# Loading a chunk's inputs with one DMA per tensor into padded rows, in a gated linear attention with a maxout layer

## The chip, the cores and the metric

The kernel runs on one core of a Trainium2 chip. The metric is the time of one execution on the device in microseconds (us). Engines are named as in the profile: PE is TensorE (PEld its weight loads), DVE is VectorE, ACT is ScalarE, POOL is GpSimd, and SP is the queue from which all DMAs here are issued.

## The reference

The inputs are q, k, v and f_logit of shape (4, 8, 768, 48): batch, heads, time, head size. All are float32. The output is 3072 x 384.

```
f = sigmoid(f_logit)
for t in range(768):
    state = f[t][:, None] * state + outer(k[t], v[t])     # 48 x 48 per batch and head
    y[t]  = q[t] @ state
x   = y with the heads side by side                        # 3072 x 384
out = maximum(x @ w1, x @ w2) @ w_out                      # d_ff = 1024
```

## The kernel before, in words

Time is cut into 6 chunks of 128 steps. One chunk of one batch is a unit. Units are numbered i = 4 * chunk + batch, so there are 24, and the four batches of a chunk follow each other. All eight heads of a unit are worked on together, with time on the 128 partitions and 8 x 48 = 384 values in a row.

The stages of a unit are functions. `s_ell` takes the logarithm of the gate (two activations on ACT, tile `e` from `ft`, then `ell`) and casts v to bf16 (tile `vb` from `vt`, on DVE). `s_cum` sums the logarithms along time with a matmul (`cum`), takes exponentials (`ei`, `ed`, `fl` on ACT), and scales k and q with them on POOL (`kp`, `qp`). `s_tr` transposes kp and qp on PE and copies them out of PSUM on DVE (`trs`). `s_a` multiplies k with q per head on PE and masks the product on DVE (`am`). `s_y` updates the state (`sa` on PE, `tmp` on DVE, `st` on POOL) and computes y on PE, which ACT copies (`x`). `s_xT` transposes x for the dense layers (`xT`, copied on DVE).

The dense layers are written as max(a, b) = b + relu(a - b). So `d` is x times (w1 - w2), `gT` its relu on ACT, and `o` sums x times (w2 w_out) and gT times w_out. DVE copies o to `ob`, which has three buffers, and SP writes it out (line 178). This work is a list of small pieces that the unit loop takes from between its stages, four per iteration and two more in the early ones. The pieces of a chunk are put on the list when the chunk's last xT is done. The preparation of the weights (`w_h`, `wo`, `w2T`, `w2o`, `wd`) stands first on the same list.

The unit loop runs over i from -4 to 23. In iteration i it does `s_y(i)`, `s_tr(i + 2)`, `s_a(i + 1)`, `s_cum(i + 3)`, `s_xT(i)` and `s_ell(i + 4)`. The order of instructions on each engine is the order in which the program writes them. A manual schedule is set, so no planner moves them. An engine that waits holds up everything behind it.

The loads of a unit are four DMAs on SP, for f, k, q and v, of 192 KB each. The pool `loads` has five buffers for each tensor, so it holds five units. Before the loop the program issues units 0 to 2, the weights w2 and w_out, unit 3, w1, and unit 4. In the loop, `load(i + 8)` stands at the end of iteration i and reuses the buffers of unit i + 3. Each load first waits until the last reader of its buffer is done: e for f, kp for k, qp for q, vb for v. The output DMAs are in the same queue, in program order.

Of the kernel before, what the change touches and what calls it, by code (L numbers as in the profile page):

```python
# [11 lines left out]
F32 = mybir.dt.float32  # L12
BF16 = mybir.dt.bfloat16
AF = mybir.ActivationFunctionType
# [3 lines left out]
def kernel(  # L18
# [14 lines left out]
    nc = tc.nc  # L33
    B, H, S, D = q.shape
    C = 128
    nch = S // C
# [4 lines left out]
    DP = 64  # L41
    NP = H // 2
    T = nch * B
# [1 line left out]

    ctx.enter_context(tc.manual_schedule())
    consts = ctx.enter_context(tc.tile_pool(name="consts", bufs=1))
    loads = ctx.enter_context(tc.tile_pool(name="loads", bufs=5))
    work = ctx.enter_context(tc.tile_pool(name="work", bufs=2))
    ps_s = ctx.enter_context(tc.tile_pool(name="ps_s", bufs=3, space=bass.MemoryType.PSUM))  # L50
    ps_a = ctx.enter_context(tc.tile_pool(name="ps_a", bufs=1, space=bass.MemoryType.PSUM))
# [2 lines left out]
    nc.scalar.preload_act_table_set("natural_log_exp_and_others")  # L54


    ld = {}

    def load(i):
        c, b = divmod(i, B)  # L60
        sl = slice(c * C, (c + 1) * C)
        t = {}
        for name, src in (("f", f_logit), ("k", k), ("q", q), ("v", v)):
            t[name] = loads.tile([C, H, D], F32, name=f"{name}t", tag=f"{name}t")
            nc.sync.dma_start(out=t[name], in_=src[b, :, sl, :].rearrange("h p d -> p h d"))
        ld[i] = t

    w1_f = consts.tile([C, JG, d_ff], F32, name="w1_f")
    w2_f = consts.tile([C, JG, d_ff], F32, name="w2_f")
# [2 lines left out]
    for i in range(3):  # L72
        load(i)
    nc.sync.dma_start(out=w2_f, in_=moe_w2.rearrange("(j p) ff -> p j ff", p=C))
    nc.sync.dma_start(out=wo_f, in_=moe_w_out.rearrange("(j p) dm -> p j dm", p=C))
    load(3)
    nc.sync.dma_start(out=w1_f, in_=moe_w1.rearrange("(j p) ff -> p j ff", p=C))
    load(4)


    ut = consts.tile([C, C], BF16)
# [104 lines left out]
    def unit(n=1):  # L186
        for _ in range(n):
            if units:
                units.popleft()()


    st = {}

    def s_ell(i):
        t = ld[i]
        e = work.tile([C, dm], F32, name="e", tag="e")
        ell = ell_b[i % 2]
        nc.scalar.activation(e, t["f"].rearrange("p h d -> p (h d)"), AF.Exp, scale=-1.0)
        nc.scalar.activation(ell[:, :, 0:D], e.rearrange("p (h d) -> p h d", h=H), AF.Ln, bias=1.0)  # L199
        vb = work.tile([C, dm], BF16, name="vb", tag="vb", bufs=6)  # L200
        nc.vector.tensor_copy(vb, t["v"].rearrange("p h d -> p (h d)"))  # L201
        st[i] = {"ell": ell, "v": vb}

    def s_cum(i):
        s, t = st[i], ld[i]
        ell = s["ell"]
        ps = ps_s.tile([C, 512], F32, name="cum", tag="s")
        nc.tensor.matmul(out=ps[:, 0:dm], lhsT=ut, rhs=ell[:, :, 0:D], start=True, stop=True)  # L208
        for p in range(NP):
            nc.tensor.matmul(out=ps[:, dm + p:dm + p + 1],  # L210
                             lhsT=ell[:, 2 * p:2 * p + 2, :].rearrange("p h d -> p (h d)"),
                             rhs=ones_col, start=True, stop=True)
        ed = work.tile([C, dm], F32, name="ed", tag="ed")
        ei = work.tile([C, dm], F32, name="ei", tag="ei")
        fl = work.tile([C, NP], F32, name="fl", tag="fl", bufs=5)
        nc.scalar.activation(ei, ps[:, 0:dm], AF.Exp)  # L216
        nc.scalar.activation(ed, ps[:, 0:dm], AF.Exp, scale=-1.0)  # L217
        nc.scalar.activation(fl, ps[:, dm:dm + NP], AF.Exp, scale=-1.0)
        qp, kp = qp_b[i % NQ], kp_b[i % NQ]
        nc.gpsimd.tensor_mul(kp[:, :, 0:D], t["k"], ei.rearrange("p (h d) -> p h d", h=H))  # L220
        nc.gpsimd.tensor_mul(qp[:, :, 0:D], t["q"], ed.rearrange("p (h d) -> p h d", h=H))  # L221
        s.update(fl=fl, qp=qp, kp=kp)
        del ld[i]

    def s_tr(i):
        s = st[i]
        ps = ps_s.tile([C, 2, NP, C], BF16, name="tr", tag="s")
        for n, src in enumerate((s["kp"], s["qp"])):
            for p in range(NP):
                nc.tensor.transpose(out=ps[:, n, p, :],  # L230
                                    in_=src[:, 2 * p:2 * p + 2, :].rearrange("p h d -> p (h d)"),
                                    identity=ident)
        tr = work.tile([C, 2, NP, C], BF16, name="trs", tag="trs", bufs=3)
        nc.vector.tensor_copy(tr, ps)  # L234
        s["tr"] = tr

    def s_a(i):
        s = st[i]
        tr = s["tr"]

        ps = ps_a.tile([C, 2, NP, C], F32, name="a", tag="a")
        for p in range(NP):
            for o in range(2):
                r = slice(o * DP, o * DP + D)
                nc.tensor.matmul(out=ps[:, o, p, :], lhsT=tr[r, 0, p, :], rhs=tr[r, 1, p, :],  # L245
                                 start=True, stop=True)
        am = work.tile([C, 2, NP, C], BF16, name="am", tag="am")
        nc.vector.tensor_mul(am.rearrange("p o n c -> p (o n) c"),  # L248
                             ps.rearrange("p o n c -> p (o n) c"), mask)
        s["am"] = am  # L250

    def s_y(i):
        c, b = divmod(i, B)
        s = st[i]
        am, vb, tr = s["am"], s["v"], s["tr"]
        old, new = st_b[b][c % 2], st_b[b][(c + 1) % 2]
        if c < nch - 1:
            sa = ps_s.tile([C, NP, 2 * D], F32, name="sa", tag="s")
            for p in range(NP):
                nc.tensor.matmul(out=sa[:, p, :],  # L260
                                 lhsT=s["kp"][:, 2 * p:2 * p + 2, :].rearrange("p h d -> p (h d)"),
                                 rhs=vb[:, 2 * p * D:(2 * p + 2) * D], start=True, stop=True)
            tmp = work.tile([C, NP, 2 * D], F32, name="tmp", tag="tmp")
            nc.vector.tensor_add(tmp, sa, old)  # L264
            for o in range(2):
                r, e = slice(o * DP, (o + 1) * DP), slice(o * D, (o + 1) * D)
                nc.gpsimd.tensor_mul(new[r, :, e], tmp[r, :, e],  # L267
                                     s["fl"][r, :].unsqueeze(2).to_broadcast([DP, NP, D]))
        y = ps_s.tile([C, dm], F32, name="y", tag="s")
        for p in range(NP):  # L270
            if c > 0:
                nc.tensor.matmul(out=y[:, 2 * p * D:(2 * p + 2) * D], lhsT=tr[:, 1, p, :],  # L272
                                 rhs=old[:, p, :], start=True, stop=False)
            for o in range(2):
                h = 2 * p + o
                ds = slice(h * D, (h + 1) * D)
                nc.tensor.matmul(out=y[:, ds], lhsT=am[:, o, p, :], rhs=vb[:, ds],  # L277
                                 start=(c == 0), stop=(c == 0 or o == 1))
        x = work.tile([C, dm], BF16, name="x", tag="x")
        nc.scalar.copy(x, y)  # L280
        s["x"] = x

    def s_xT(i):
        c, b = divmod(i, B)
        s = st.pop(i)
        if b == 0:
            xT_g[c] = work.tile([C, JG, GT], BF16, name="xT", tag="xT", bufs=3)
        ps = ps_s.tile([C, JG, C], BF16, name="xtp", tag="s")
        for j in range(JG):
            nc.tensor.transpose(out=ps[:, j, :], in_=s["x"][:, j * C:(j + 1) * C], identity=ident)  # L290
        nc.vector.tensor_copy(xT_g[c][:, :, b * C:(b + 1) * C], ps)  # L291


    for i in range(-4, T):
        if i >= 0:
            s_y(i)
        unit()
        if 0 <= i + 2 < T:
            s_tr(i + 2)
        unit()  # L300
        if 0 <= i + 1 < T:
            s_a(i + 1)
        unit()
        if 0 <= i + 3 < T:
            s_cum(i + 3)
        unit()
        if i >= 0:
            s_xT(i)
        if i < B:
            unit()  # L310
            unit()
        if i >= 0 and i % B == B - 1:
            push_group(i // B)
        if 0 <= i + 4 < T:
            s_ell(i + 4)
        if 5 <= i + 8 < T:
            load(i + 8)
    while units:
        unit()

# [29 lines left out]
```

## Time and profile before

| what | value |
|---|---|
| median of 2 timed runs | 186.99 us (186.93 to 187.04) |
| profiled execution | 185.38 us |
| its span, first to last instruction | 183.6 us |
| mean granted TensorE clock | 0.944 |
| busy: PE, DVE, ACT, POOL | 138.6, 102.5, 86.1, 75.7 us |
| DMA: packets, bytes | 105154 packets, 28.56 MB, of which 100272 under 512 B |

All times in the lines of the profile count from the start of the span. The timed runs give the whole execution. The profiled execution has 1.8 us around its span. A line number such as L201 is that of the kernel before.

The lines of the changed kernel are shifted by 11 to 13. For example, the cast of v stands in line 201 before and in line 213 after.

### The profile page before, as it was taken

What the parts mean: (1) busy time and instruction counts of PE and PEld (TensorE: products, weight loads), DVE (VectorE), ACT (ScalarE), POOL (GpSimd) and SP (SyncE); (2) the same over time, 40 slices, a digit from 0 to 9 for tenths busy, and PEclk for the clock granted to TensorE, in tenths of its full rate; (3) what the DMA queues carried; (4) which work ended last, traced back from release to release, by engine and by line L of the source; (5) the groups of instructions that cost most, each with busy time, mean ns of one, the idle gap of its engine ahead of it and who ended that gap; (6) DMA issues with size and microseconds to landing.
All of it is one profiled execution on the core that took longest, in us unless ns stands there. A gap on an engine that the chain in (4) does not pass through costs nothing.

```text
span 183.6 us, 3633 instructions
## 1 busy us (share of the span) xinstructions
PE 138.6 (75%) x1373; PEld 85.4 (46%) x1384; DVE 102.5 (56%) x161; ACT 86.1 (47%) x200; POOL 75.7 (41%) x107
## 2 busy tenths in 40 slices
PE   0000208946778989999999998999899988998992
PEld 0000106534555545655456654665556654564560
DVE  8200605389777576686676676766776744452031
ACT  2000074483555675446744577346873376412700
POOL 8200004646666366544466544566544644000000
PEclk9999999985555999999999999999999999999999
DMA  6999999999999997698996999969801120022022
GB/s 114 194 185 347 373 199 362 186 187 171 194 189 190 164 191 131 165 209 174 195 151 164 215 172 186 172 142 216 152 0 43 50 86 0 4 87 86 0 89 86
DMA packets 105154, 28.56 MB, mean 156 GB/s; under 512 B 100272, under 2 KB 104368, under 8 KB 105136
## 3 DMA queue, kind: packets, MB, share of 16 engines
q1 hardware_dynamic: 105136, 28.32, 77.1%
q8 instruction: 11, 0.18, 0.5%
q14 instruction: 7, 0.06, 0.1%
HBM read 23.59 MB, written 4.72 MB: 154 GB/s over the span
## 4 chain that ended last, share of the span: by engine, by line
issue 39%; PE 32%; POOL 23%; ACT 3%; POOLq 1%; DVE 1%; ACTq 0%
PE o L172 13%; POOL qp L221 11%; POOL kp L220 9%; PE d L156 9%; PE tr L230 6%; PE a L245 2%; POOL st L98 1%; ACT ei L216 1%; PE y L272 1%; ACT ed L217 1%; PE y L277 1%; ACT gT L158 1%; POOLq L345 1%; POOL ell L94 0%; PE cum L208 0%
## 5 line engine op out<-in xcount | busy, mean ns | idle before, releaser
L220 POOL TENSOR_TENSOR kp<-kt,ei 128x384 bf16<-128x384 f32 x24 | 24.9, 1036 | 76.4 <-issue 38.9
L156 PE MATMUL d<-xT,wd 128*128 128x512 bf16 x133 | 36.7, 383 | 2.3 <-DVE xT L291 1.1
L158 ACT ACTIVATE gT<-d 128x512 bf16<-128x512 f32 x48 | 29.0, 605 | 19.0 <-PE d L156 18.5
L172 PE MATMUL o<-wo,gT 128*128 128x384 bf16 x192 | 37.7, 326 | 0.0
L234 DVE COPY trs<-tr 128x1024 bf16<-128x1024 bf16 x24 | 16.6, 692 | 25.8 <-PE tr L230 25.7
L248 DVE TENSOR_TENSOR am<-a,mask 128x1024 bf16<-128x1024 f32 x24 | 29.3, 1219 | 2.9 <-PE a L245 2.9
L216 ACT ACTIVATE ei<-cum 128x384 f32<-128x384 f32 x24 | 11.7, 489 | 38.2 <-PE cum L210 38.2
L221 POOL TENSOR_TENSOR qp<-qt,ed 128x384 bf16<-128x384 f32 x24 | 27.6, 1148 | 0.0
L176 DVE COPY ob<-o 128x384 f32<-128x384 f32 x24 | 13.4, 558 | 23.3 <-PE o L172 22.4
L172 PEld LDWEIGHTS <-gT 128*128 128x128 bf16 x192 | 17.8, 98 | 10.4
L267 POOL TENSOR_TENSOR st<-tmp,fl 64x192 bf16<-64x192 f32 x40 | 20.0, 501 | 2.3 <-DVE tmp L264 0.8
L124 PE MATMUL w2tp<-ident,w_h 128*128 128x128 bf16 x24 | 3.5, 308 | 21.0 <-DVE w_h L112 21.0
L201 DVE CAST vb<-vt 128x384 bf16<-128x384 f32 x24 | 16.9, 703 | 0.0
L156 PEld LDWEIGHTS <-wd 128*128 128x128 bf16 x144 | 11.8, 98 | 10.8 <-issue 2.3
L172 PE MATMUL o<-w2o,xT 128*128 128x384 bf16 x72 | 15.7, 327 | 0.0
L230 PE MATMUL tr<-ident,qp 128*128 128x128 bf16 x96 | 10.6, 239 | 5.8 <-POOL qp L221 5.0
L277 PE MATMUL y<-vb,am 128*128 128x48 bf16 x192 | 12.0, 190 | 2.2 <-DVE am L248 1.4
L116 ACT CAST wo<-wo_f 128x768 bf16<-128x768 f32 x4 | 3.1, 824 | 21.9 <-DMA wo_f<-in_moe_w_out_dram 21.9
L208 PE MATMUL cum<-ell,ut 128*128 128x384 bf16 x24 | 8.9, 369 | 6.0 <-ACT ell L199 6.0
L277 PEld LDWEIGHTS <-am 128*128 128x128 bf16 x192 | 10.3, 101 | 6.4 <-DVE xT L291 3.7
L280 ACT CAST x<-y 128x384 bf16<-128x384 f32 x24 | 11.2, 467 | 4.2 <-PE y L277 4.1
L199 ACT ACTIVATE ell<-e 128x384 bf16<-128x384 f32 x24 | 12.5, 523 | 0.9
(42 smaller groups left out, 185.1 us busy)
## 6 DMA issues: line engine op xcount, KB each, us to landing
ft<-in_f_logit_dram SPq DMA_DIRECT2D x24, 192.0 KB, 4.3
kt<-in_k_dram SPq DMA_DIRECT2D x24, 192.0 KB, 4.2
qt<-in_q_dram SPq DMA_DIRECT2D x24, 192.0 KB, 4.2
vt<-in_v_dram SPq DMA_DIRECT2D x24, 192.0 KB, 4.3
out_dram<-ob SPq DMA_DIRECT2D x24, 192.0 KB, 2.0
w_f<-in_moe_w_dram SPq DMA_DIRECT2D x2, 1536.0 KB, 7.7
wo_f<-in_moe_w_out_dram SPq DMA_DIRECT2D x1, 1536.0 KB, 11.0
```

The source lines that it names most:

```text
L156: nc.tensor.matmul(out=ps, lhsT=wd[:, j, f * C:(f + 1) * C], rhs=xT[:, j, :], start=(j == 0), stop=(j == JG - 1))
L158: nc.scalar.activation(gT[:, f, :], ps, AF.Relu)
L172: nc.tensor.matmul(out=ps, lhsT=mms[n][0], rhs=mms[n][1], start=(n == 0), stop=(n == len(mms) - 1))
L201: nc.vector.tensor_copy(vb, t["v"].rearrange("p h d -> p (h d)"))
L216: nc.scalar.activation(ei, ps[:, 0:dm], AF.Exp)
L220: nc.gpsimd.tensor_mul(kp[:, :, 0:D], t["k"], ei.rearrange("p (h d) -> p h d", h=H))
L221: nc.gpsimd.tensor_mul(qp[:, :, 0:D], t["q"], ed.rearrange("p (h d) -> p h d", h=H))
L230: nc.tensor.transpose(out=ps[:, n, p, :], in_=src[:, 2 * p:2 * p + 2, :].rearrange("p h d -> p (h d)"), identity=ident)
L234: nc.vector.tensor_copy(tr, ps)
L248: nc.vector.tensor_mul(am.rearrange("p o n c -> p (o n) c"), ps.rearrange("p o n c -> p (o n) c"), mask)
L267: nc.gpsimd.tensor_mul(new[r, :, e], tmp[r, :, e], s["fl"][r, :].unsqueeze(2).to_broadcast([DP, NP, D]))
L277: nc.tensor.matmul(out=y[:, ds], lhsT=am[:, o, p, :], rhs=vb[:, ds], start=(c == 0), stop=(c == 0 or o == 1))
```

## The change

The tiles of f, k, q and v now hold a whole chunk of all four batches, `[C, B, H, DP]`. DP is 64, so each row of 48 float32 values (192 bytes) lies in a slot of 256 bytes. The pool has two buffers for each tensor, two chunks in place of five units.

Chunk 0 is still loaded in four parts, unit by unit, in the old places among the weights. Every later chunk is loaded by `load_chunk` with one DMA for each tensor, in the order f, k, q, v. Each has 128 partitions x 32 rows x 48 values, 768 KB. Chunk 1 is issued after w1, where the load of unit 4 was. Chunk c + 2 is issued at the end of iteration 4c, the first of chunk c, and uses the buffers of chunk c. The compute instructions are the same in number and order on every engine. They read the tiles through views with a gap after each row of 48.

On SP the DMAs now stand in this order: chunk 0 and the weights, chunks 1, 2 and 3, four outputs, chunk 4, four outputs, chunk 5, and sixteen outputs.

```diff
-    loads = ctx.enter_context(tc.tile_pool(name="loads", bufs=5))
+    loads = ctx.enter_context(tc.tile_pool(name="loads", bufs=2))
...
-    ld = {}
+    SRC = (("f", f_logit), ("k", k), ("q", q), ("v", v))
+    ld_c = {n: {} for n, _ in SRC}
+
+    def load_one(name, src, c):
+        if c not in ld_c[name]:
+            ld_c[name][c] = loads.tile([C, B, H, DP], F32, name=f"{name}t", tag=f"{name}t")
+        return ld_c[name][c]
 
     def load(i):
         c, b = divmod(i, B)
         sl = slice(c * C, (c + 1) * C)
-        t = {}
-        for name, src in (("f", f_logit), ("k", k), ("q", q), ("v", v)):
-            t[name] = loads.tile([C, H, D], F32, name=f"{name}t", tag=f"{name}t")
-            nc.sync.dma_start(out=t[name], in_=src[b, :, sl, :].rearrange("h p d -> p h d"))
-        ld[i] = t
+        for name, src in SRC:
+            t = load_one(name, src, c)
+            nc.sync.dma_start(out=t[:, b, :, 0:D], in_=src[b, :, sl, :].rearrange("h p d -> p h d"))
+
+    def load_chunk(c):
+        sl = slice(c * C, (c + 1) * C)
+        for name, src in SRC:
+            t = load_one(name, src, c)
+            nc.sync.dma_start(out=t[:, :, :, 0:D].rearrange("p b h d -> p (b h) d"),
+                              in_=src[:, :, sl, :].rearrange("b h p d -> p (b h) d"))
...
-    load(4)
+    load_chunk(1)
...
     def s_ell(i):
-        t = ld[i]
+        c, b = divmod(i, B)
+        t = {n: ld_c[n][c][:, b, :, 0:D] for n in ld_c}
...
-        nc.scalar.activation(e, t["f"].rearrange("p h d -> p (h d)"), AF.Exp, scale=-1.0)
+        nc.scalar.activation(e.rearrange("p (h d) -> p h d", h=H), t["f"], AF.Exp, scale=-1.0)
...
-        nc.vector.tensor_copy(vb, t["v"].rearrange("p h d -> p (h d)"))
+        nc.vector.tensor_copy(vb.rearrange("p (h d) -> p h d", h=H), t["v"])
...
-        if 5 <= i + 8 < T:
-            load(i + 8)
+        if i >= 0 and i % B == 0 and i // B + 2 < nch:
+            load_chunk(i // B + 2)
```

More of the change, by code (lines that the diff above doesn't have):

```diff
@@ L194, in s_ell @@
     def s_ell(i):
-        t = ld[i]
+        c, b = divmod(i, B)
+        t = {n: ld_c[n][c][:, b, :, 0:D] for n in ld_c}
         e = work.tile([C, dm], F32, name="e", tag="e")
         ell = ell_b[i % 2]
-        nc.scalar.activation(e, t["f"].rearrange("p h d -> p (h d)"), AF.Exp, scale=-1.0)
+        nc.scalar.activation(e.rearrange("p (h d) -> p h d", h=H), t["f"], AF.Exp, scale=-1.0)
         nc.scalar.activation(ell[:, :, 0:D], e.rearrange("p (h d) -> p h d", h=H), AF.Ln, bias=1.0)
         vb = work.tile([C, dm], BF16, name="vb", tag="vb", bufs=6)
-        nc.vector.tensor_copy(vb, t["v"].rearrange("p h d -> p (h d)"))
+        nc.vector.tensor_copy(vb.rearrange("p (h d) -> p h d", h=H), t["v"])
         st[i] = {"ell": ell, "v": vb}
     def s_cum(i):
-        s, t = st[i], ld[i]
+        c, b = divmod(i, B)
+        s = st[i]
+        t = {n: ld_c[n][c][:, b, :, 0:D] for n in ld_c}
         ell = s["ell"]
@@ L222, in s_cum @@
         s.update(fl=fl, qp=qp, kp=kp)
-        del ld[i]
     def s_tr(i):
```

## The prediction

> **What bounds the kernel now.** I read the views in this order: the slices and the table of DMA issues on the page, to see whether the loads are the limit; the busy times by stretch, to see which engine limits each stage; the timelines of the queue that issues DMAs, of VectorE, GpSimd and ScalarE between 43 and 53 us, because that is where a load of a whole chunk would first be late; last the landing times of single loads.
>
> ```profile
> PEclk9999999985555999999999999999999999999999
> DMA  6999999999999997698996999969801120022022
> GB/s 114 194 185 347 373 199 362 186 187 171 194 189 190 164 191 131 165 209 174 195 151 164 215 172 186 172 142 216 152 0 43 50 86 0 4 87 86 0 89 86
> ...
> vt<-in_v_dram SPq DMA_DIRECT2D x24, 192.0 KB, 4.3
> out_dram<-ob SPq DMA_DIRECT2D x24, 192.0 KB, 2.0
> ```
>
> One slice is 183.6/40 = 4.59 us. The DMA engines are full for the first 15 slices (to 69 us) and fairly busy up to slice 28. PEclk is at half in slices 9 to 12 (41 to 60 us). So the loads could be the limit early, but busy is not the same as late. The stretches tell which stage is held by what (columns: length, busy time and instructions of PE, PEld, DVE, ACT, POOL, then clock, DMA share, GB/s):
>
> ```profile
> 32.00:36.50 4.50, 4.50 (x29) 2.65 (x28) 1.89 (x4) 1.90 (x5) 2.82 (x2) 1.00 1.25 186
> 50.00:54.50 4.50, 3.40 (x37) 2.34 (x36) 3.41 (x6) 2.23 (x7) 3.02 (x5) 0.50 1.39 193
> 75.00:97.50 22.50, 21.20 (x230) 13.05 (x230) 15.13 (x24) 13.40 (x34) 12.20 (x16) 1.00 0.94 175
> ```
>
> From 75 us on TensorE is busy for 21.20 of 22.50 us: this stage, four units (one chunk) long, is TensorE's, and loads only have to keep up. Between 41 and 59 us no engine is full. There the unit loop has a period of 4.51 us (kp starts at 44.69, 49.19 and, one period on, 53.70) and is a ring: kp and qp on GpSimd, their transposes on TensorE, cum behind them in TensorE's order, ei on ScalarE, and the next kp. These lines (start, length, and in brackets the idle time before and its releaser) are the end of unit iteration 0 and the beginning of iteration 1:
>
> ```profile
> 44.69 0.35 DVE L291 COPY xT<-xtp 128x384 bf16<-128x384 bf16 x1
> 44.95 0.95 DVE L201 CAST vb<-vt 128x384 bf16<-128x384 f32 x1
> 45.82 0.55 DVE L264 TENSOR_TENSOR tmp<-sa,st 128x384 f32<-128x384 f32 x1
> 47.45 0.69 DVE L234 COPY trs<-tr 128x1024 bf16<-128x1024 bf16 x1 [1.08 <-PE tr L230]
> ...
> 46.72 1.07 POOL L267 TENSOR_TENSOR st<-tmp,fl 64x192 bf16<-64x192 f32 x2
> 49.19 1.00 POOL L220 TENSOR_TENSOR kp<-kt,ei 128x384 bf16<-128x384 f32 x1 [1.40 <-issue]
> ...
> 44.87 0.54 ACT L198 ACTIVATE e<-ft 128x384 f32<-128x384 f32 x1
> ```
>
> The cast vb at 44.95 is that of unit 4, the first unit of chunk 1 (four casts stand before it in DVE's order). It waits for nothing. When did its data come? The issue list and the landing times answer:
>
> ```profile
> 24.43 0.99 SPq L77 DMA_DIRECT2D w_f<-in_moe_w_dram  x1
> ...
> 31.79 0.76 SPq L65 DMA_DIRECT2D vt<-in_v_dram  x1
> ...
> 45.12 0.70 SPq L65 DMA_DIRECT2D vt<-in_v_dram  x1
> ```
>
> The load of w1 issued at 24.43 landed 7.7 us later, at 32.1. The v of unit 4 (31.79) took 4.5 us: 36.3. The v of unit 7 (45.12) took 3.8: 48.9. Between 32.1 and 48.9 just the 16 loads of units 4 to 7 land, 16.8/16 = 1.05 us each, back to back (192 KB in 1.05 us is 187 GB/s, the rate in the stretches). So unit 4 has its four tensors 8.6 us before the cast, because the loads are ordered by unit.
>
> **What the Trainium skill says.** "DMA: Bandwidth & Descriptors", section "Queues, rings and completion order": on each DMA engine descriptors are consumed in ring order. The trace agrees, landings follow issues one by one at 1.05 us. The same page, section "How a descriptor splits into AXI transactions": a piece that doesn't start on a multiple of 256 bytes can need one transaction more. The page counts 100,272 packets under 512 bytes; runs stay 192 bytes long after the change, and the HBM side keeps its steps of 192 bytes, so only the SBUF side becomes aligned; no run here shows what that is worth. "VectorE: DVE Perf Modes", section "Mode 2×_2P": a one-source copy in SBUF keeps two elements a cycle if the outermost dimension is even; 8 heads are even, so the cast from padded rows should keep its 349 ns minimum. "TensorE: Matmul & The Clock Gate", Part 1: the clock comes back after a busy window of about 3.4 us that runs free of the kernel. Here it came back at about 60.5 us, 1.3 us after the d matmuls started at 59.22.
>
> **The change part by part.**
>
> Padding: the same packets, the same bytes. ACT reads 8x48 with gaps; ell, already written with gaps in that shape, takes 523 ns against 535 for e. GpSimd walks 8x48 already. I take zero for all engine instructions. For the DMA I take the same 1.05 us per 192 KB; bounds below.
>
> Chunk 0 stays four loads per tensor in the same order, w2, wo, w1 too. Up to 32.1 us nothing moves.
>
> Chunk 1 (the first real effect): 3,072 KB in the order f, k, q, v, 4.2 us each, behind w1. Landings: f 36.3, k 40.5, q 44.7, v 48.9. Wanted (starts in the trace): e of unit 4 at 44.87 (f 8.6 us early), kp at 49.19 (k early), qp at 50.15 (q early), vb at 44.95: v is 4.0 us late. VectorE stops there. Queued behind it are tmp of unit 1, trs of unit 3, am of unit 2. With GpSimd idle then, vb takes 0.35 instead of 0.95. So vb 49.0 to 49.35, tmp to 49.9, and st on GpSimd, which stands before kp in its order, goes 49.9 to 51.0 instead of 46.72 to 47.79. The idle 1.40 us before kp is used up, and kp of unit 4 starts at 51.0 instead of 49.19: **+1.8 to 1.9 us**. VectorE's backlog doesn't add to it: trs 49.9 to 50.5, am to 51.8, y of unit 2 on TensorE to 52.8, before qp of unit 4 is done at 53.1. From there the ring runs its old period. The delay persists: TensorE has no backlog of d and o work before 59 us, and is full afterwards.
>
> Chunk 2: issued when e, kp, qp and vb of unit 3 are done (by 46.8), so the ring doesn't run dry: lands 48.9 + 16.8 = 65.7 (the old kernel's unit 11 landed v at 62.4 + 3.7 = 66.1). First want: vb of unit 8 at 64.23 + 1.9 = 66.1. Just in time, zero taken, at most 0.5.
>
> Chunk 3: lands at 82.5 to 83, wanted by vb of unit 12 at 86.63 + 1.9. Chunk 4: on SP it stands behind the four output DMAs of group 0, the last issued at 81.69 + 1.9 = 83.6; with 16.8 us and a 2 us latency it lands at 102.5, wanted at 110.8. Chunk 5 the same, 125 against 133. Zero each.
>
> Outputs: now queued behind 3 MB. The first of group 0 (issued 73.47 + 1.9) waits for chunk 3 until about 83 and lands near 85. The fourth ob copy (81.11 + 1.9 = 83.0) needs that buffer (three ob buffers): a stall of up to 2 us on VectorE. Behind it stand tmp and trs with 0.88 idle before trs, and GpSimd idles 2.29 us before its next kp. I take 0.2 for the groups together; bound 0 to 1.
>
> Sum: 1.9 + 0.2 = 2.1 us. The profiled execution took 185.38 (span 183.6 and 1.8 around it), so 187.5; the median of the runs shown is 186.99, 1.6 above, so **189.0 us** (1% slower). I let the 1.6 stand for such things as the phase of the clock window.
>
> **The rivals.**
>
> *The wait is absorbed* (20%): v lands a little earlier, or unprofiled runs reach vb later than 44.95. For: 1.4 us of slack before kp, and the timed runs are 1.6 us longer. Against: it would take 2 us. 187.0.
>
> *The clock comes back a window later* (18%): d work starts 1.9 us later, at 61.1. If the window that ended at 60.5 counts as idle now, the half clock lasts 3.4 us longer. About 10 of the 12 d matmuls of that iteration then start 427 ns apart instead of 216 (the cold and warm spacings for 512 columns on the same page of the skill, an estimate): +2.1. 186.99 + 2.1 + 2.1 = 191.2.
>
> *Large requests leave gaps* (7%): the first load from an idle queue took 3.2 us, 2.1 more than in the stream. If each 768 KB request waits for its predecessor, chunk 1's v is 4 x 2.1 = 8.4 us later: 197. Against: w2 and wo, 1,536 KB each, run at 347 to 373 GB/s in their slices, so large requests do stream.
>
> *Faster* (5%): aligned writes make each packet cheaper. The place is the start, which waits for data: ScalarE waits 21.9 us for wo, with twelve 192 KB loads (12.5 us) ahead of it. Gaining 3.7 us, 2%, takes packets about 30% cheaper; the stall at v then goes as well, v landing at 38. Time: 183. Against: 1,536-byte output rows and 192-byte rows differ by size as a fixed cost would have it, and the reads keep their odd starts.
>
> **How the numbers follow.** Likeliest case 50% at 189.0; absorbed 20%; late clock 18%; gaps 7%; faster 5%. The range 186.5 to 192.0 holds the first three. The line of 2%, about what a measurement of this kernel can tell from no change, lies at 183.3 and 190.7: faster 5%; slower the late clock, the gaps and a small part of the likeliest case, 26%; the rest, 69%, within.
>
> **What would show it.** In the new profile: vb of unit 4 near 49 us with 3 to 4 us of idle before it, released by the load of v; kp of unit 4 at 51; from then on every mark about 2 us later; the clock's return between 60 and 64; chunk loads 16.8 us long; no wait on e, kp or qp for a load after 32 us. Wrong if the loads ahead of w1 land visibly earlier than 23.9 for wo, if a second vb (units 8, 12, 16) waits over 1 us, or if ob waits for its output DMA more than 2 us.

## The result, and the profile after

| | before | changed | ratio |
|---|---|---|---|
| median | 186.99 us | 200.63 us (199.77 and 201.5) | 1.073 (1.053 to 1.093) |
| profiled execution | 185.38 us | 199.77 us | |
| its span | 183.6 us | 198.0 us | |
| granted clock | 0.944 | 0.922 | |

The change costs 7%, where 1% was forecast. The measured time lies far outside the range. The page of the changed kernel shows the main reason in its rows of slices:

```profile
PEclk9999999985555599999699999999999999999999
DMA  7999999999999999998979979999400121013022
GB/s 117 164 163 330 361 185 338 163 163 167 163 163 163 167 165 167 166 163 189 174 115 163 167 177 177 165 163 156 160 3 0 52 74 40 0 43 114 5 82 81
```

The DMA row has the same nines as before in the first slices. The row below it has not: where the kernel before mostly moved 185 to 199 GB/s in the early slices of small packets, this one moves 163 to 167. It does so from slice 1 on, in the first loads, which are still single units. At 164 GB/s each 192 KB (196.6 thousand bytes) takes 1.20 us instead of 1.05. The busy time by stretch says it more exactly (before, then changed; the last two columns are DMA share and GB/s):

```profile
5.00:11.00 6.00, 0.00 (x0) 0.00 (x0) 0.89 (x1) 0.00 (x0) 0.61 (x2) 1.00 1.32 191
```

```profile
5.00:11.00 6.00, 0.00 (x0) 0.00 (x0) 0.89 (x1) 0.00 (x0) 0.61 (x2) 1.00 1.51 164
```

The timelines of the changed kernel show where the late data hurts. Its line numbers are 11 to 14 higher than before: kp stands in L220 before and in L234 after. First, VectorE at the first unit of chunk 1 and GpSimd behind it:

```profile
46.67 0.35 DVE L304 COPY xT<-xtp 128x384 bf16<-128x384 bf16 x1
54.18 0.36 DVE L213 CAST vb<-vt 128x384 bf16<-128x384 f32 x1 [7.16 <-DMA vt<-in_v_dram]
54.45 0.55 DVE L277 TENSOR_TENSOR tmp<-sa,st 128x384 f32<-128x384 f32 x1
...
55.08 1.08 POOL L280 TENSOR_TENSOR st<-tmp,fl 64x192 bf16<-64x192 f32 x2 [6.46 <-DVE tmp L277]
56.24 1.00 POOL L234 TENSOR_TENSOR kp<-kt,ei 128x384 bf16<-128x384 f32 x1
```

This is the predicted wait, in the predicted place and passed on by the predicted chain (vb, tmp, st, kp), but 7.16 us long where 4 were expected. One more cast waits for its load, that of unit 8, for 0.98 us. It adds nothing: kp of units 8 to 10 starts 8.1 to 8.2 us later than before, as kp of unit 7 does. Second, the fourth output of a group, behind the loads of chunk 3:

```profile
87.29 1.21 DVE L261 TENSOR_TENSOR am<-a,mask 128x1024 bf16<-128x1024 f32 x1
92.25 0.56 DVE L187 COPY ob<-o 128x384 f32<-128x384 f32 x1 [3.75 <-DMA out_dram<-ob]
92.73 0.35 DVE L304 COPY xT<-xtp 128x384 bf16<-128x384 bf16 x1
...
93.13 0.81 PE L167 MATMUL d<-xT,wd 128*128 128x512 bf16 x3 [3.09 <-DVE xT L304]
```

The ob copy needs the buffer of an output whose DMA is queued behind the loads. It stands before xT in VectorE's order, and TensorE needs that xT for its d work. So TensorE stood still for 3.09 us. The same happens twice more: ob waits 2.00 us until 117.05 and 2.23 us until 140.51, and TensorE then stands for 1.33 and 1.56 us. Third, the clock:

```profile
66.30:69.90 3.60, 3.60 (x21) 1.65 (x21) 1.36 (x3) 1.26 (x4) 2.02 (x3) 0.50 1.32 168
90.00:93.80 3.80, 0.71 (x6) 0.31 (x4) 1.55 (x4) 0.79 (x2) 1.11 (x2) 1.00 0.65 188
93.90:97.20 3.30, 3.30 (x22) 1.57 (x20) 1.28 (x2) 1.20 (x2) 0.99 (x2) 0.50 1.17 191
```

The column before the DMA share is the granted clock. The first d work begins at 66.3 us and runs at half clock for 3.6 us, against 1.3 us before. After the stretch from 90 to 93.8 us, in which TensorE was busy for only 0.71 us, the clock goes back to half for 3.3 us, with TensorE full.

The starts of kp, the first link of the ring, give the sum:

| kp of unit | before | changed | later by | what was added in between |
|---|---|---|---|---|
| 0 | 28.50 | 29.87 | 1.4 | w_out lands at 25.3 instead of 23.9 |
| 3 | 44.69 | 46.67 | 2.0 | the matmuls for w2o take 5.19 us instead of 4.57: 0.6 |
| 4 | 49.19 | 56.24 | 7.1 | wait of vb for v: 5.1 |
| 7 | 64.09 | 72.27 | 8.2 | half clock under the first d work: 1.1 |
| 11 | 86.38 | 98.84 | 12.5 | wait of ob for its output, and the clock's second fall: 4.3 |
| 15 | 108.67 | 122.07 | 13.4 | second wait of ob: 0.9 |
| 19 | 130.96 | 145.52 | 14.6 | third wait of ob: 1.2 |

The spans differ by 14.4 us. The amounts are differences between two executions. What each step is put down to is read from the timelines; the experiments test the load rate, the order and the output wait, but not the half clock by itself.

### The profile page after: what moved, and what is told of

Same layout as the page of the kernel before. It is cut to its first block, busy times and chain, and to the rows that moved or that the text cites. A ratio compares the mean times of both kernels' runs of the same rounds, so it can differ in the third digit from the quotient of the medians.

```text
span 198.0 us, 3513 instructions
## 1 busy us (share of the span) xinstructions
PE 142.0 (72%) x1384; PEld 86.5 (44%) x1384; DVE 101.6 (51%) x161; ACT 86.1 (44%) x200; POOL 75.1 (38%) x107
## 4 chain that ended last, share of the span: by engine, by line
PE 38%; issue 23%; POOL 16%; DMA 12%; ACT 6%; DVE 1%; POOLq 1%; DVEq 0%; ACTq 0%
PE o L183 14%; PE d L167 13%; DMA out_dram<-ob 12%; POOL qp L235 7%; POOL kp L234 6%; PE tr L243 5%; PE a L258 4%; ACT ei L230 4%; POOL st L109 1%; ACT gT L169 1%; PE y L285 1%; ACT ed L231 1%; PE cum L222 1%; PE y L290 1%; DVE xT L304 1%
## 5 line engine op out<-in xcount | busy, mean ns | idle before, releaser
L234 POOL TENSOR_TENSOR kp<-kt,ei 128x384 bf16<-128x384 f32 x24 | 24.9, 1036 | 78.6 <-ACT ei L230 69.6
L167 PE MATMUL d<-xT,wd 128*128 128x512 bf16 x144 | 40.0, 397 | 7.1 <-DVE xT L304 7.1
L187 DVE COPY ob<-o 128x384 f32<-128x384 f32 x24 | 13.4, 557 | 28.9 <-PE o L183 20.0
L235 POOL TENSOR_TENSOR qp<-qt,ed 128x384 bf16<-128x384 f32 x24 | 26.8, 1116 | 0.0
L213 DVE CAST vb<-vt 128x384 bf16<-128x384 f32 x24 | 16.0, 667 | 8.1 <-DMA vt<-in_v_dram 8.1
L210 ACT ACTIVATE e<-ft 128x384 f32<-128x384 f32 x24 | 13.0, 541 | 0.0
## 6 DMA issues: line engine op xcount, KB each, us to landing
qt<-in_q_dram SPq DMA_DIRECT2D x5, 768.0 KB, 12.5
vt<-in_v_dram SPq DMA_DIRECT2D x5, 768.0 KB, 12.5
```

Of the source, the lines that this page charges most:

```text
L167: nc.tensor.matmul(out=ps, lhsT=wd[:, j, f * C:(f + 1) * C], rhs=xT[:, j, :], start=(j == 0), stop=(j == JG - 1))
L213: nc.vector.tensor_copy(vb.rearrange("p (h d) -> p h d", h=H), t["v"])
```

## The experiments

Theory A was that a 192-byte packet costs more when it is written into rows 256 bytes apart, and that all else follows from late data. Rival B was that the large requests or the new order of the queue make the loads slow.

**Padding alone.** This is the kernel before with padded tiles of one unit. The two instructions that read f and v take the views with gaps (not shown here).

```diff
-            t[name] = loads.tile([C, H, D], F32, name=f"{name}t", tag=f"{name}t")
+            t[name] = loads.tile([C, H, DP], F32, name=f"{name}t", tag=f"{name}t")[:, :, 0:D]
```

> The kernel before with one thing changed: every load tile has rows of 64 places instead of 48 (256 bytes apart instead of 192), still one unit per tile and five buffers. Theory A (a 192-byte packet costs more when the rows it writes lie 256 bytes apart, whatever the size of the request): a 192 KB load takes 1.20 us instead of 1.05, w_out lands at about 25.3 instead of 23.9 us, kp of unit 0 starts at about 29.9 instead of 28.5, and as units are loaded far ahead nothing else waits: 188 to 189 us. Rival B (the slow loads come from the large requests or from the order of the queue): 1.05 us per load and 187 us.

Measured: 187.65 us, ratio 1.0069 (1.0043 to 1.0095). The loads run at the changed kernel's rate, with requests of the old size:

```profile
5.00:11.00 6.00, 0.00 (x0) 0.00 (x0) 0.00 (x0) 0.00 (x0) 0.89 (x3) 1.00 1.50 163
```

w_out lands at 25.3 us (14.3 + 11.0) and kp of unit 0 starts at 29.88. No load of f, k, q or v is waited for in the loop, because units are loaded far ahead. So the padding slows the loads, and by itself it costs little: it needs the rest of the change to do the larger harm. The time is a little under the 188 expected.

**Chunks without padding.**

```diff
-            ld_c[name][c] = loads.tile([C, B, H, DP], F32, name=f"{name}t", tag=f"{name}t")
+            ld_c[name][c] = loads.tile([C, B, H, D], F32, name=f"{name}t", tag=f"{name}t")
```

> The changed kernel with the rows of a chunk's tile left 192 bytes apart (no padding); chunk requests, order f, k, q, v and two buffers stay. Theory A: a 768 KB request takes 4.2 us instead of 4.8, v of chunk 1 lands at 48.9 instead of 54.2, vb of unit 4 waits 4 instead of 7.2 us, the fourth ob copy of group 0 waits at most 2 us: 189 to 190.5 us, what the prediction had for the whole change. Rival B: requests stay at 4.8 us and the time at 198 to 201 us.

Measured: 188.87 us, ratio 1.0113 (1.0044 to 1.0182). VectorE, then GpSimd, around the first unit of chunk 1:

```profile
45.92 0.35 DVE L304 COPY xT<-xtp 128x384 bf16<-128x384 bf16 x1
49.76 0.36 DVE L213 CAST vb<-vt 128x384 bf16<-128x384 f32 x1 [3.49 <-DMA vt<-in_v_dram]
...
45.91 1.00 POOL L234 TENSOR_TENSOR kp<-kt,ei 128x384 bf16<-128x384 f32 x1 [0.53 <-POOL st L280]
...
51.82 0.99 POOL L234 TENSOR_TENSOR kp<-kt,ei 128x384 bf16<-128x384 f32 x1
```

The kp period across the wait is 51.82 - 45.91 = 5.91 us, 1.4 more than 4.51. The loads of chunk 1 are quick again. From 36 to 44 us, changed kernel first, then dense rows:

```profile
36.00:44.00 8.00, 4.67 (x54) 3.05 (x52) 4.82 (x5) 4.70 (x11) 3.77 (x4) 0.92 1.52 163
36.00:44.00 8.00, 4.37 (x53) 2.96 (x51) 5.58 (x6) 4.21 (x10) 2.93 (x2) 0.90 1.35 197
```

Large requests in the new order are not slow by themselves, so rival B is refuted. In time, dense rows cost about the 2 us that the prediction gave the whole change (the interval allows 0.8 to 3.4). The trace does not give all of it to the wait for v: kp of unit 3 starts 1.2 us later than before already (45.91 against 44.69), as the matmuls for w2o take 5.74 us in this execution against 4.57. Why they do is open; in the run below with dense rows, v second and seven buffers they take 4.57 again.

**Seven output buffers.**

```diff
-                ob = work.tile([C, dm], F32, name="ob", tag="ob", bufs=3)
+                ob = work.tile([C, dm], F32, name="ob", tag="ob", bufs=7)
```

> The changed kernel with seven instead of three buffers for ob, so that an ob copy never waits for the output DMA that stands behind a chunk's loads. Theory: the waits of ob for its output (8.0 us in three waits, of which 5.4 and about 2 stop TensorE through xT) are on the path: 5 to 7 us less, 194 to 196 us, and the granted clock does not fall a second time at 94 us. Rival: the wait is only moved, to the load of chunk 2 or 3 (v of unit 8 or 12), and less than 2 us are won.

Measured: 192.89 us, ratio 1.035 (1.0276 to 1.0425), which is 7.7 us below the changed kernel (the profiled spans differ by 7.1). The waits of ob for its output are gone, and the fourth copy waits 0.80 us for TensorE as in the kernel before:

```profile
88.58 0.56 DVE L187 COPY ob<-o 128x384 f32<-128x384 f32 x1 [0.80 <-PE o L183]
```

The output waits on the loads in front of it in the queue, and about half of the loss was there. The gain is a little over the 5 to 7 expected. The clock's second fall is gone too: after 69 us it stays at full.

**v as the second request.**

```diff
-        for name, src in SRC:
+        for name, src in (SRC[0], SRC[3], SRC[1], SRC[2]):
```

> The changed kernel with the requests of a chunk in the order f, v, k, q instead of f, k, q, v. v of chunk 1 lands at 43.6 and vb of unit 4 does not wait at 46.9; q lands last, at 54.2, and qp of unit 4 waits until then: kp of unit 4 at about 51 instead of 56, the next transposes about 3 us earlier than in the changed kernel. Theory: the three microseconds won there are lost again, since the fourth ob copy still waits until the loads of chunk 3 have passed at about 92 us: 199 to 201 us. Rival: the waits add up independently, 197.5 us.

Measured: 199.54 us, ratio 1.07 (1.0634 to 1.0766). That is not clearly faster than the changed kernel, whose two runs took 199.77 and 201.5; the profiled spans are 197.8 and 198.0. kp of unit 4 starts at 51.76 instead of 56.24, and in place of vb only qp waits for its load, 1.78 us. But at the fourth output VectorE now stands for twice as long:

```profile
84.64 1.22 DVE L261 TENSOR_TENSOR am<-a,mask 128x1024 bf16<-128x1024 f32 x1
92.94 0.56 DVE L187 COPY ob<-o 128x384 f32<-128x384 f32 x1 [7.08 <-DMA out_dram<-ob]
```

The copy starts at 92.94 against 92.25: the end of the load stream sets it, and what is won earlier is waited away here, as expected.

**v second and seven output buffers, rows padded; the same with dense rows.** The first run combines the edits of the last two. The second also takes the rows to 192 bytes.

> The changed kernel with the order f, v, k, q and seven ob buffers, rows still 256 bytes apart. Left are the start (+1.4 us) and the wait of qp of unit 4 for q (+1.8 us), and perhaps a later return of the clock (up to 2): 189.5 to 191.5 us. With seven ob buffers the gain of the order, which was lost when it was made alone (199.5 us against 200.6), should now count: at least 2 us below the 192.9 of the run with seven ob buffers alone. Rival: the order never matters, 192 to 193 us.

> The changed kernel without padding, with the order f, v, k, q and with seven ob buffers: all three causes named so far taken away, chunk requests and two buffers kept. If they are all, the time is that of the kernel before, 186.5 to 188 us (q of chunk 1 lands at about 49.5 and qp of unit 4 wants it at about 50). If the large requests cost something by themselves, 188.5 us or more.

Measured: padded 189.94 us, ratio 1.0206 (1.0134 to 1.0278); dense 186.68 us, ratio 1.0002 (0.997 to 1.0033). The order, which alone won nothing clear of the scatter, is worth about 3 us (192.89 to 189.94) once the output wait is out of the way. With all three causes removed no difference is left, within 0.3%: chunk requests and two buffers cost nothing by themselves, and they bring nothing either.

**Loads alone, by the distance of the rows.** A kernel of loads only, in groups of twelve. It leaves out all compute and writes two of the 24 blocks of the output. It ran once.

> Only loads: all compute is left out and only two of the 24 output blocks are written. Groups of twelve 192 KB loads (128 partitions x 8 rows x 48 values), each group into rows at another distance: rowsa 192 bytes (dense), rowsb 208, rowsc 224, rowsd 256, rowse 288, rowsf 320, rowsg 384, rowsh 512, rowsi dense but begun 64 bytes later. Then the same with every fourth time step, so that every source row starts at the same place of a 256-byte line: rowsj (source at 0, rows dense), rowsk (source at 0, rows 256 apart), rowsl (source at 192, dense), rowsm (source at 192, rows 256 apart). Theory G (any gap between the rows costs, as rows that adjoin are written together): rowsa, rowsi, rowsj, rowsl at 1.05 us a load, all others at 1.20. Theory P (the distance of 256 bytes itself is what costs, rows falling on the same places): only rowsd, rowsh, rowsk, rowsm at 1.20, the others at 1.05. Theory S (the read side sets the price): rowsj and rowsk faster than rowsl and rowsm whatever the rows of the target.

The busy times by stretch, one stretch inside each group's transfers, in the order rowsa to rowsm. The columns are length, GpSimd's busy time, clock, DMA share and GB/s:

```profile
6.00:12.00 6.00, 0.00 (x0) 1.00 1.02 203
20.00:28.00 8.00, 0.00 (x0) 1.00 1.20 195
32.00:39.00 7.00, 0.00 (x0) 1.00 1.29 202
45.00:54.00 9.00, 0.00 (x0) 1.00 1.53 163
58.00:65.00 7.00, 0.00 (x0) 1.00 1.36 200
70.00:76.00 6.00, 0.00 (x0) 1.00 1.16 210
81.00:88.00 7.00, 0.00 (x0) 1.00 1.04 201
95.00:103.00 8.00, 0.00 (x0) 1.00 1.51 163
108.00:114.00 6.00, 0.00 (x0) 1.00 1.08 213
119.00:125.00 6.00, 0.00 (x0) 1.00 1.02 209
132.00:140.00 8.00, 0.00 (x0) 1.00 1.51 164
145.00:151.00 6.00, 0.00 (x0) 1.00 1.14 213
158.00:165.00 7.00, 0.00 (x0) 1.00 1.53 163
```

All four groups with rows 256 or 512 bytes apart run at 163 or 164 GB/s (rowsd, rowsh, rowsk, rowsm). All nine others run at 195 to 213, gaps or no gaps (208, 224, 288, 320 and 384 bytes), and for dense rows begun 64 bytes later or not. Where the source rows start makes no difference: with the source always at 0 or always at 192 of a 256-byte line, 209 and 213 dense, 164 and 163 at 256 apart. Theory P stands as far as the distance goes; G and S fall. The size of the tile is not the cause: the dense chunk tiles take 6,144 bytes of a partition, a multiple of 2,048 like the padded ones, and load quickly. In the slow groups all rows of a partition begin at the same place of a 256-byte line. Whether it matters which place that is was not tried, as only dense rows were also begun 64 bytes later.

**One number.** The changed kernel with rows 224 bytes apart.

```diff
-            ld_c[name][c] = loads.tile([C, B, H, DP], F32, name=f"{name}t", tag=f"{name}t")
+            ld_c[name][c] = loads.tile([C, B, H, 56], F32, name=f"{name}t", tag=f"{name}t")
```

> The changed kernel with one number changed: rows 224 bytes apart (56 places) instead of 256. Padding, gaps, chunk requests, order and buffers stay. If the distance of 256 bytes is what costs (rows 224 apart took 0.98 us a load where rows 256 apart took 1.20), the time falls to that of the dense chunk run, 187.5 to 190 us, with v of chunk 1 landing near 49 instead of 54 us. If it is the gap, 199 to 201 us.

Measured: 186.78 us, ratio 1.0002 (0.9966 to 1.0038), a little better than expected. 13.9 us of difference (200.63 to 186.78) hang on eight places per row. The request for v of chunk 1 keeps SP for 3.85 us against 4.75 in the changed kernel, vb of unit 4 waits 2.72 us, and no ob copy waits for an output. So v still comes last and late here. The kp period across the wait is 5.13 us, 0.6 over 4.51, and the median shows no loss.

**The start.** As padding alone had moved the whole kernel by the delay of w_out, the order of the first loads was changed in the kernel before.

```diff
-    for i in range(3):
-        load(i)
+    load(0)
     nc.sync.dma_start(out=w2_f, ...)
     nc.sync.dma_start(out=wo_f, ...)
-    load(3)
+    load(1)
     nc.sync.dma_start(out=w1_f, ...)
-    load(4)
+    for i in range(2, 5):
+        load(i)
```

> The kernel before with another order of the loads before the loop: unit 0, w2, w_out, unit 1, w1, units 2, 3, 4 (before: units 0, 1, 2, w2, w_out, unit 3, w1, unit 4). The runs with padding showed that the start waits for data: later landings of w_out moved everything by as much. w_out then lands at about 15.5 instead of 23.9 us and w1 at 24 instead of 32; units 2, 3 and 4 then land at 28, 32.5 and 36.7, one per 4.2 us against a loop of 4.5. Theory: the chain starts up to 8 us earlier, 179 to 182 us. Rival: units 2 to 4 come too late, or the clock is at half longer, and less than 3 us are won.

Measured: 180.21 us, ratio 0.9689 (0.9614 to 0.9763), faster than both kernels. ScalarE's wait for w_out falls from 21.9 to 13.9 us:

```profile
ACT wo L116 <- DMA wo_f<-in_moe_w_out_dram: 13.9, 1, 13.9
```

kp of unit 0 starts at 20.52 instead of 28.50, as expected. At kp of unit 6 all 8 us are still there (50.00 against 58.23), at unit 7 it is 6.2 (57.93 against 64.09): in between, from 52 to 56 us, d work runs at half clock. Then the same with rows 320 bytes apart:

> The kernel with the weights loaded earlier (180.2 us) and rows of its one-unit tiles 320 bytes apart (80 places), the distance with the quickest loads of the padded groups (0.92 us against 1.05 for dense rows in the kernel before). If that rate holds here, w_out and w1 land up to 1 us sooner: 179 to 180 us. Rival: dense rows are as quick at this place (0.94 in the run of loads alone) and nothing is won: 180 to 180.6 us.

Measured: 180.09 us, ratio 0.9642 (0.9616 to 0.9668). The stretch from 4 to 20 us shows 292 GB/s against 287, and w_out lands within 0.1 us of the run before. The rival holds: nothing clear of the scatter is won.

## Why the prediction was wrong

**The failed step is "For the DMA I take the same 1.05 us per 192 KB".** It measured 1.20 us. The bound was drawn on one side only: aligned writes could make packets cheaper, and a rival stood for that, but nothing stood for padding that makes them dearer. The Trainium skill ("DMA: Bandwidth & Descriptors", section "How a descriptor splits into AXI transactions") lets a piece that does not start on a multiple of 256 bytes need more transactions, so it pointed the same way. The runs show no such price for the source rows: 213 GB/s from 192, 209 from 0 of a 256-byte line. No load of the kernel before wrote rows 256 bytes apart, so nothing in its profile could price them, and both ends were needed. A cost of 14% more per load, put through the same sums, gives v of chunk 1 at about 34.0 (the landing of w1) + 4 x 4.8 = 53.2 us, close to the 54.1 measured. It also turns the stall at the outputs, "up to 2 us" with 0.2 taken, into waits that stop TensorE. That the rate is the cause and not only a companion is shown by the run with rows 224 bytes apart, which takes all 13.9 us back.

**The mechanism of the order was right.** v last in its chunk, VectorE held in order, tmp, st and kp behind it: the dense chunk run has all of it. That its 188.87 us meets the forecast of 189.0 is partly luck, as its trace puts 1.4 us on the wait where 1.9 were forecast, and 1.2 us on other work. With rows 224 bytes apart the wait is 2.72 us and only 0.6 us of it reaches kp, which is what the rival of the absorbed wait had described. In the changed kernel e, kp and qp never waited for a load after the start, as foreseen.

**The start.** "Up to 32.1 us nothing moves" fell with the price: w_out came 1.4 us later, and kp of unit 0 with it.

**Outputs behind loads** were named with their place, the three buffers and the fourth copy, but priced from the wrong load rate: 0.2 us with a bound of 1, where the table shows 6.4 us with the clock's second fall. An ob wait of over 2 us was among the prediction's own signs of being wrong. What the forecast left out there is xT, which stands behind ob on VectorE and feeds TensorE: it looked only at tmp and trs. The run with seven buffers shows 7.7 us for these waits and what follows from them.

**The clock.** The rival of a later return came true besides (1.1 us at kp of unit 7), and a second fall after TensorE's halt at 90 us was not foreseen. With seven output buffers neither the halt nor the fall is there.

**Casts and activations from padded rows** cost nothing, as taken: vb keeps its 349 ns minimum, and the median of e is 535 ns in both kernels.

**The other rivals.** Large requests leave no gaps that cost time: with rows dense, v second and seven buffers the kernel takes 186.68 us. The faster case, cheaper packets at the start, has the right lever with the wrong sign: the start does wait for data, as the run with another order of loads shows.

## What to carry to other kernels

The rate at which rows of 192 bytes were loaded into on-chip memory depended on the distance of the rows there: measure it for a layout before padding to a round number, and give an unmeasured cost a bound on both sides. Slower loads that are issued far ahead cost little (0.7%), but with two chunk buffers, a tensor that comes last in its batch and stores queued behind the loads, the same slowness cost 7%. Before a saving is counted, look for the next wait that is set by the same stream: the new order won nothing clear of the scatter alone and 3 us once the output wait was gone.

## What the runs showed of the hardware

Rows of 192 bytes written 256 or 512 bytes apart load at 163 to 164 GB/s in these runs, whatever the start of the source rows. At 192, 208, 224, 288, 320 and 384 bytes it is 195 to 213. Dense rows begun 64 bytes later are no slower (213). These rates of the kernel of loads come from one execution; the full kernels show 163 to 166 for 256 bytes and 186 to 202 for 192 and 224. Why the distance matters is not shown: that rows fall on the same places of the memory fits, but was not tried by itself. It also stays open why dense rows run at 203 GB/s and more in the kernel of loads alone and at 186 to 197 in the full kernels, where those 256 bytes apart run at 163 to 166 in both. The order of units and chunks differs between them, and other engines work beside the loads.
